# Two interleaved attention and gated-linear layers on one core: joint key/query weight loads, GpSimd alone for the key scaling, another engine order at the two layer changes

## The chip, the core and the metric

The kernel runs on 1 core of a Trainium2 chip. The metric is device microseconds of one execution. Five engines run their own instruction streams and meet at semaphores: TensorE (PE, with its weight loads shown as PEld), VectorE (DVE), ScalarE (ACT), GpSimd (POOL) and SyncE (SP), which issues the DMAs.

## What is computed

x is 2048 tokens by 576 features, in bf16. Two layers follow each other, with shared weights. Each is an attention half and a gated half, each behind a layer norm and with a residual:

```
qkv = ln(x) @ wqkv                       # 32 heads of 18
pq, pk = q @ w_phi, k @ w_phi            # per head
phi(p) = [softmax(p), softmax(-p)]       # 36 features per head
kv = sum over all tokens of phi_k * v ;  z = sum of phi_k
o  = (phi_q @ kv) / (phi_q @ z + 1e-6)
x  = x + o @ wo
x  = x + ((ln(x) @ w_gate) * (ln(x) @ w_up)) @ w_down      # 576 -> 4608 -> 576
```

The sum over all tokens makes a barrier in each layer: no token can get its attention output before the last token's key features are in.

## The kernel before

The tokens are 16 tiles of 128, in 8 blocks of 2. The program is recorded by a list scheduler written in Python (`Tracker`, `Sched`, lines 19 to 520): generators such as `t_ln` or `t_ain` yield groups of instructions, and the scheduler takes at each step the group with the smallest key, which is its estimated start less some constants (`bias`, `age`, `boost`). The engines then run exactly this order. Where a group may run on several engines (a request of the kind "alt"), the scheduler picks the engine that it believes will be done first.

The steps are these.

- **Head.** `t_load` loads the first tokens, `w_phi` and the raw key and query weights (`Wrawk`, `Wrawq`, five row blocks of 640 columns each). `t_fuse` transposes each row block (L954), copies it out (L957, tile `WTq`) and multiplies it by a block-diagonal of `w_phi` (L967), so that `Wk` and `Wq` give pk and pq at once. `t_flag` bounds the exponents from the Gram diagonals of the raw weights (L846, L849, L857, L863 to L866); every engine reads the flag and takes one of two programs (L231). These inputs take the fast program, which does not subtract a maximum ahead of exp.
- **Attention of layer 1.** For each tile: layer norm (`t_ln`: statistics L1007 and L1015 on DVE, the negated mean L1021, ln and exp on ACT L1023 and L1025, scaling L1036 on POOL or DVE, or L1032 on ACT), a transpose into `xT` (through PE at L1044 for the first block, through a DMA for the others), the projections to k and v (L1077), exp of p and of -p on ACT (L1198), the 64 sums on DVE (L1264), their reciprocals (two activations L1271, or L1267 on DVE), the scaling of the 1152 features by them in two halves (L1279, on POOL or on DVE), and the product with v (L1318) into two PSUM banks. `t_barrier` masks the result into `BD` (L1403).
- **Between barrier and gated half.** Tiles 0 and 1 go through the attention output (L1430 or L1439, L1460, L1468 to L1482, L1494, L1065), the layer norm and the transpose. The PE fills with query projections (`t_qproj`) of tiles 2 to 15, whose results lie in `xT` until their turn.
- **Gated half.** For each block 648 matmuls of 64 rows (L1599) and then 144 of the down projection (L1673, L1675); beside them lie the attention outputs of later blocks, and in layer 1 the keys of layer 2 for the blocks that are done (`t_ain(2, ..)`). Then the same barrier stands once more ahead of layer 2.

`proj` has two ways for a product with 576 weight rows: ten matmuls of 128 rows (L1065), or 18 of 64 rows (L1077), which go in pairs to the two halves of the array. Layer 1 takes the second way. In the second barrier the scheduler's own choice (a request "pe2") took the first.

`lend` lends feature tiles the memory of the down-projection buffers and of `hT`; so one tile carries several names (`dd`, `dd_h1g`, `dd_w3f`). The raw weights lie in memory that the gate and up weights take later (`over`), so the later loads wait for the fusing.

Of the kernel before, what the change touches and what calls it, by code (L numbers as in the profile page):

```python
# [6 lines left out]
BF16 = mybir.dt.bfloat16  # L7
# [10 lines left out]

class Tracker:
    def __init__(self):  # L20
        self.ops = {e: [] for e in ENGINES}
        self.count = {e: 0 for e in ENGINES}
        self.know = {e: {} for e in ENGINES}
        self.snap = {}
        self.fin = {}
        self.lastw = {}
        self.readers = {}
        self.lastacc = {}
        self.dma_groups = []
        self.pend_w = {}  # L30
        self.pend_r = {}
        self.stats = {"ops": 0, "waits": 0, "multiwait": 0, "pe_multiwait": 0}
# [66 lines left out]
    def _commit(self, me, eng, reads, writes, excl):  # L99
        for r in reads:  # L100
            d = self.readers.setdefault(r, {})
            if d.get(me[0], 0) < me[1]:
                d[me[0]] = me[1]
        for w in writes:
            self.lastw[w] = me
            self.readers[w] = {}
        for x in excl:
            self.lastacc.setdefault(x, {})[eng] = me[1]
# [135 lines left out]
class Op:  # L244
    __slots__ = ("dur", "emit", "reads", "writes", "excl", "mode", "order")

    def __init__(self, dur, emit, reads=(), writes=(), excl=(), mode=0, order=()):
# [9 lines left out]
class _Thread:  # L257
    __slots__ = ("gen", "prio", "req", "name", "deps_cache", "est", "t_ready", "seq", "alt", "boost", "age")
    _n = 0

    def __init__(self, gen, prio, name):
# [10 lines left out]
        self.age = 0.0  # L272


class Sched:

    def __init__(self, tracker):
        self.tr = tracker
        self.free_at = {e: 0.0 for e in ENGINES}
# [14 lines left out]
        self.hold = -1500.0  # L294
        self.alt_cost = {"dve": 1.0, "pool": 1.0, "act": 1.0}
# [17 lines left out]
    def _try_acquire(self, th):  # L313
# [4 lines left out]
        for i, t in self.pools["pb"]["rel_time"].items():  # L318
            self.pools["pb"]["rel_time"][i] = self.bank_time(i)
# [29 lines left out]
    def bank_time(self, bank):  # L349
        la = self.tr.lastacc.get(("pb", bank), {})  # L350
        return max([self.tr.fin.get(k, 0.0) for k in la.items()] + [0.0])

    def run(self):
        tr = self.tr
        while True:
# [83 lines left out]
            for th in self.threads:  # L439
                r = th.req  # L440
                if r[0] == "alt":
                    pick = None
                    for eng, ops in r[1]:
                        deps = []
                        for o in ops:
                            deps.extend(tr.deps_for(eng, o.reads, o.writes, o.excl, True, o.order))
                        e_ = max(self.free_at[eng], tr.ready_time(deps), th.t_ready)
# [5 lines left out]
                elif r[0] == "pe2":  # L453
                    ops = r[1 + self.pe_mode]
                    deps = []
                    for o in ops:
                        deps.extend(tr.deps_for("pe", o.reads, o.writes, o.excl, True, o.order))
                    est = max(self.free_at["pe"], tr.ready_time(deps, "pe"), th.t_ready)
                    th.alt = ("ops", "pe", ops, self.pe_mode)
                elif r[0] == "ops":  # L460
                    eng = r[1]
                    deps = []
                    for o in r[2]:
                        deps.extend(tr.deps_for(eng, o.reads, o.writes, o.excl, True, o.order))
                    est = max(self.free_at[eng], tr.ready_time(deps, eng), th.t_ready)
                    if eng == "pe" and r[2][0].mode != self.pe_mode:
                        est += self.pe_switch
                elif r[0] == "dma":
                    deps = tr.deps_for("sp", r[3], r[4], (), False)
                    est = max(self.free_at[r[9] if len(r) > 9 else "sp"], tr.ready_time(deps), th.t_ready)  # L470
# [3 lines left out]
                key = (est - self.bias.get(int(th.prio), 0.0) - th.age - (self.hold if late else th.boost), -th.prio)  # L474
# [8 lines left out]
            if r[0] == "ops":  # L483
# [4 lines left out]
                for o in r[2]:  # L488
# [11 lines left out]
                    t = fin  # L500
                if self.log is not None:
                    self.log.append((th.name, eng, t_beg, t, len(r[2]), self.free_at[eng]))
                self.free_at[eng] = t
            else:
# [4 lines left out]
                start = max(issue, self.dma_free[queue])  # L509
                xfer = nbytes / self.dma_bw  # L510
                self.dma_free[queue] = start + xfer
# [68 lines left out]
class K:  # L580
    def __init__(self, nc, A_x, A_wqkv, A_w_phi, A_wo, B_w_gate, B_w_up, B_w_down, out, fast, base=None):
# [10 lines left out]
        self.vlead = 9  # L592
        self.fage = 500.0
        self.fageq = 0.0
        self.fage2 = 300.0
        self.lnb = 2
        self.pes = (0, 1, 2, 3, 4, 5, 6, 7, 8, 9, 10, 11, 12, 13)
        self.early = (2, 2)
        self.pex = 1
        self.qlead = 12 if fast else 8  # L600
# [3 lines left out]
        self.lnlead = 7  # L604
# [4 lines left out]
        self.pqg = 6 if fast else 10  # L609
# [7 lines left out]
        self.fqp = 6.5  # L617
# [13 lines left out]
    def alloc(self):  # L631
# [25 lines left out]
        self.Wraw = {"k": AT("Wrawk", [128, 5, 640], BF16, wg0 + 6 * FF), "q": AT("Wrawq", [128, 5, 640], BF16, wu0 + 6 * FF)}  # L657
        self.WTq = AT("WTq", [128, 5, 5, 128], BF16, wu0 + 4 * FF)
# [29 lines left out]
        self.over = {("g", 3): [("Wraw", "k", kt) for kt in range(5)], ("u", 3): [("Wraw", "q", kt) for kt in range(5)], ("u", 2): [("WTq", i) for i in range(6)]}  # L688

    def lend(self):  # L690
# [63 lines left out]
        self.g_ot = [g("ot%d" % i) for i in range(self.NOT)]  # L754

# [78 lines left out]
    def t_flag(self):  # L834
# [5 lines left out]
        for i, which in enumerate("kq"):  # L840
            W = s.Wraw[which]
            gots = yield ("acqn", ["pb"], 2)
            banks = [g_[1] for g_ in gots]
            for kt in range(5):
                yield ("wait", ("ld", "raw", which, kt))
                yield ("ops", "pe", [Op(60, (lambda e, m=m, kt=kt, W=W, bank=banks[m // 3], c=128 * (m % 3), st=(kt == 0 and m in (0, 3)): e.matmul(  # L846
                    s.ps[:, bank, c:c + 128], W[:, kt, 128 * m:128 * m + 128], W[:, kt, 128 * m:128 * m + 128], start=st, stop=(kt == 4), skip_group_check=True)),
                    reads=[("Wraw", which, kt)], writes=[("pbd", banks[m // 3])], excl=[("pb", banks[m // 3])]) for m in range(5)])
            yield ("ops", "dve", [Op(d_dve(n), (lambda e, c=c, bank=bank, n=n: e.tensor_reduce(s.cst[:, c:c + 1], s.ps[:, bank, 0:n], AX.X, ALU.max)),  # L849
                                     reads=[("pbd", bank)], writes=[("cst", c)], excl=[("pb", bank)]) for c, bank, n in ((1, banks[0], 384), (2, banks[1], 256))]  # L850
                   + [Op(70, (lambda e: e.tensor_tensor(s.cst[:, 1:2], s.cst[:, 1:2], s.cst[:, 2:3], ALU.max)), reads=[("cst", 1), ("cst", 2)], writes=[("cst", 1)]),
                      Op(70, (lambda e, c=i: (e.tensor_copy(s.cst[:, 3:4], s.cst[:, 1:2]) if c == 0 else e.tensor_tensor(s.cst[:, 1:2], s.cst[:, 1:2], s.cst[:, 3:4], ALU.max))),
                         reads=[("cst", 1), ("cst", 3)], writes=[("cst", 3 if i == 0 else 1)])])
            for bank in banks:
                yield ("rel", "pb", bank)
        (_, bank), = yield ("acqn", ["pb"], 1)
        yield ("ops", "pe", [Op(250, (lambda e, c=c: e.matmul(s.ps[0:1, bank, 128 * c:128 * c + 128], s.cst[:, c:c + 1], s.identf[:], start=(c == 0), stop=(c == 1), skip_group_check=True)),  # L857
                                reads=[("cst", c), ("identf",)], writes=[("pbd", bank)], excl=[("pb", bank)]) for c in range(2)])
# [4 lines left out]
            Op(330, (lambda e: e.tensor_reduce(s.flg[0:1, 0:2], s.ps[0:1, bank, 0:256].rearrange("p (c n) -> p c n", c=2), AX.X, ALU.max)), reads=[("pbd", bank)], writes=[("flg", 0)], excl=[("pb", bank)]),  # L863
            Op(70, (lambda e: e.tensor_tensor(s.flg[0:1, 2:3], s.flg[0:1, 0:1], s.flg[0:1, 0:1], ALU.mult)), reads=[("flg", 0)], writes=[("flg", 1)]),
            Op(70, (lambda e: e.tensor_tensor(s.flg[0:1, 3:4], s.flg[0:1, 2:3], s.flg[0:1, 1:2], ALU.mult)), reads=[("flg", 0), ("flg", 1)], writes=[("flg", 2)]),
            Op(70, (lambda e: e.tensor_scalar(s.flag[0:1, 0:1], s.flg[0:1, 3:4], lim, None, ALU.is_lt)), reads=[("flg", 2)], writes=[("flag",)])])  # L866
# [4 lines left out]
    def t_load(self):  # L871
# [15 lines left out]
        def rawload(kt, queue="sp", which="k"):  # L887
            n = 128 if kt < 4 else 64
            c0 = D if which == "k" else 0
            return grp("raw%s%d" % (which, kt), [((lambda e, p=p: e.dma_start(s.Wraw[which][p:p + n, kt, :], wqkv[128 * kt:128 * kt + n, c0:c0 + 640])),  # L890
                                       [("Wraw", which, kt)], n * 640 * 2) for p in range(0, 128, n)], ("ld", "raw", which, kt), queue)

        yield from xload(0)
# [10 lines left out]
        def side():  # L904
            yield from grp("wphi5", items, ("ld", "wphi5"), "act")
            yield from rawload(1, "act")
            yield from rawload(3, "act")

        yield ("go", side(), 9, "side")
        yield from rawload(0)  # L910
        yield from rawload(2)
        yield from rawload(4)
        for kt in range(5):
            yield from rawload(kt, "sp", "q")
# [25 lines left out]
    def t_fuse(self, which):  # L940
        s = self
        Wm, km = (s.Wq, "Wq") if which == "q" else (s.Wk, "Wk")
        yield ("wait", "bdphi")
        yield ("age", s.fage if which == "k" else s.fageq)
        for kt in range(5):
            yield ("wait", ("ld", "raw", which, kt))
            if which == "q":
                yield ("wait", "branch")
                if not s.fast:
                    yield ("wait", ("ain", 1, s.fq + s.fqs * kt))  # L950
            if True:
# [998 lines left out]
```

## Time and profile before

| what | value |
|---|---|
| runs shown, median (lowest to highest of 3) | 1084.21 us (1083.66 to 1086.02) |
| the profiled execution's own time | 1083.22 us |
| its span, first to last instruction | 1081.5 us |
| PE busy | 1055.8 us, 98% |
| DVE, ACT, POOL busy | 487.3, 353.6, 198.6 us |
| first matmul of the gated half, layer 1 | at 104.56 us |
| last down projection of layer 1, first gated matmul of layer 2 | about 594.8 us, 625.74 us |
| granted TensorE clock, mean | 0.997 |

A window's row gives start and end, its length, then for PE, PEld, DVE, ACT and POOL the busy microseconds with the number of instructions in brackets, then the granted clock, the share of the DMA engines and GB/s. A row of the timeline gives start, duration, engine, line, operation, what is written from what, and the engine's idle time before it with what ended it. A row of the groups gives the count, the busy time with the mean duration in ns, and the idle time before.

### The profile page before, as it was taken

The page shows a single profiled execution, that of the slowest core. Times are in us where ns is not written, and L with a number is a line of the kernel's source. Part 1 is how long each engine was busy: PE and PEld are TensorE (multiplying, and loading weights), DVE is VectorE, ACT ScalarE, POOL GpSimd, SP SyncE. Part 2 cuts the span into 40 slices and gives each one's busy share as a digit, 9 for nine tenths or more (in the row PEclk, how much of TensorE's full clock was granted, in tenths as well). Part 3 has the DMA queues.
Part 4 walks back from the last instruction along what each step waited for, and adds up shares of the span by engine and source line. Part 5 has one row for each costly group of instructions (what it writes and reads, how often), then busy time and mean ns, then how long its engine had stood idle before and what let it go on. Part 6 is the DMA issues. An engine that isn't in the chain of part 4 may idle for free.

```text
span 1081.5 us, 34135 instructions
## 1 busy us (share of the span) xinstructions
PE 1055.8 (98%) x15678; PEld 807.8 (75%) x15678; DVE 487.3 (45%) x978; ACT 353.6 (33%) x846; POOL 198.6 (18%) x226
## 2 busy tenths in 40 slices
PE   6998999999999999999999999999999999999997
PEld 4666868879686877868686787777868686868684
DVE  5995626444453635425232644443424343424131
ACT  5786323314241432315141743131313131203030
POOL 3453003122130403103020220101010101000000
PEclk9999999999999999999999999999999999999999
DMA  5689155180835436183605133627190808180604
GB/s 141 120 220 289 37 144 127 54 192 15 219 40 176 83 100 149 33 200 37 199 14 165 45 47 83 175 61 196 37 220 21 237 15 232 25 221 15 209 2 146
DMA packets 179705, 128.18 MB, mean 119 GB/s; under 512 B 98016, under 2 KB 178400, under 8 KB 178400
## 3 DMA queue, kind: packets, MB, share of 16 engines
q1 hardware_dynamic: 178656, 125.55, 46.0%
q8 instruction: 125, 2.05, 0.8%
q10 hardware_dynamic: 896, 0.35, 0.1%
q14 instruction: 28, 0.23, 0.1%
HBM read 100.90 MB, written 2.36 MB: 95 GB/s over the span
## 4 chain that ended last, share of the span: by engine, by line
PE 90%; DVE 6%; DMA 2%; ACT 1%; issue 0%; POOL 0%; ACTq 0%
PE ps L1599 52%; PE ps L1673 22%; PE ps L1077 8%; PE ps L1675 3%; PE ps L1065 2%; DVE ss_w4f L1264 1%; DMA wdx<-in_B_w_down_dram 1%; PE ps L1460 1%; DVE dd_h1g L1279 1%; DVE st L1007 1%; PE ps L1318 1%; DMA wdr<-in_B_w_down_dram 0%; DMA Wrawk<-in_A_wqkv_dram 0%; DVE dd_w3f L1279 0%; DVE xln L1036 0%
## 5 line engine op out<-in xcount | busy, mean ns | idle before, releaser
L1599 PE MATMUL ps<-xT,Wg 64*128 64x256 bf16 x4608 | 582.9, 269 | 0.0
L1599 PE MATMUL ps<-xT,Wu 64*128 64x256 bf16 x4608 | 581.3, 269 | 0.2 <-DVE dd L1482 0.2
L1599 PEld LDWEIGHTS ps<-xT,Wu 64*128 64x128 bf16 x4608 | 431.7, 94 | 28.0 <-DVE dd L1482 0.4
L1599 PEld LDWEIGHTS ps<-xT,Wg 64*128 64x128 bf16 x4608 | 430.4, 94 | 28.7 <-issue 3.3
L1648 DVE TENSOR_TENSOR hT<-ps,hT 128x512 bf16<-128x512 f32 x288 | 199.2, 692 | 309.4 <-ACT hT L1646 309.4
L1646 ACT CAST hT<-ps 128x512 bf16<-128x512 f32 x288 | 168.6, 586 | 407.2 <-PE ps L1599 396.3
L1673 PE MATMUL ps<-wdr,hT 128*128 128x512 bf16 x960 | 244.5, 380 | 0.8 <-DMA wdr<-in_B_w_down_dram 0.5
L1279 POOL TENSOR_TENSOR dd<-dd,ss 128x576 bf16<-128x576 bf16 x94 | 111.2, 1210 | 456.6 <-ACT ss L1275 447.9
L1675 PE MATMUL ps<-wdr,hT 128*128 128x64 bf16 x960 | 184.9, 193 | 0.0
L1673 PEld LDWEIGHTS ps<-wdr,hT 128*128 128x128 bf16 x960 | 93.8, 98 | 112.0 <-DMA wdr<-in_B_w_down_dram 2.1
L1599 PE MATMUL ps<-xT,Wr 64*128 64x256 bf16 x1152 | 170.6, 269 | 0.0
L1036 POOL TENSOR_SCALAR xln<-x_sb,nmean,rstd 128x64 bf16<-128x64 bf16 (+1 forms) x98 | 60.1, 618 | 301.1 <-DVE nmean L1021 182.6
L1716 DVE TENSOR_TENSOR x_sb<-ps,x_sb 128x64 bf16<-128x64 f32 x32 | 7.0, 218 | 227.4 <-PE ps L1675 227.4
L1675 PEld LDWEIGHTS ps<-wdr,hT 128*128 128x128 bf16 x960 | 94.1, 98 | 0.2
L1275 ACT ACTIVATE ss<-ss 128x64 f32<-128x64 f32 x92 | 23.8, 259 | 193.1 <-DVE ss L1264 192.2
L1264 DVE TENSOR_REDUCE ss<-dd 128x64 f32<-128x1152 bf16 x48 | 63.6, 1346 | 23.7 <-ACT dd L1198 22.1
L1599 PEld LDWEIGHTS ps<-xT,Wr 64*128 64x128 bf16 x1152 | 66.9, 94 | 6.2
L1673 PE MATMUL ps<-wdx,hT 128*128 128x512 bf16 x192 | 54.4, 380 | 0.7 <-DMA wdx<-in_B_w_down_dram 0.5
L1077 PE MATMUL ps<-Wv,xT 64*128 64x288 bf16 x540 | 47.8, 287 | 3.2 <-DVE flag L866 1.3
L1077 PE MATMUL ps<-Wk,xT 64*128 64x288 bf16 x540 | 47.6, 287 | 1.2 <-ACT dd_w3f L1198 0.8
L1007 DVE BATCH_NORM_STATS2 st<-x_sb 128x6 f32<-128x288 bf16 x120 | 46.3, 444 | 0.7 <-DVE flag L866 0.7
L1077 PE MATMUL ps<-Wo,oT 64*128 64x288 bf16 x504 | 40.2, 283 | 0.0
(129 smaller groups left out, 752.1 us busy)
## 6 DMA issues: line engine op xcount, KB each, us to landing
wdr<-in_B_w_down_dram SPq DMA_DIRECT2D x240, 288.0 KB, 3.7
wdx<-in_B_w_down_dram SPq DMA_DIRECT2D x48, 288.0 KB, 3.8
Wg<-in_B_w_gate_dram SPq DMA_DIRECT2D x4, 1152.0 KB, 13.6
Wu<-in_B_w_up_dram SPq DMA_DIRECT2D x4, 1152.0 KB, 15.9
x_sb<-in_A_x_dram SPq DMA_DIRECT2D x8, 288.0 KB, 4.4
out_dram<-x_sb SPq DMA_DIRECT2D x16, 144.0 KB, 2.4
xT<-xln SPq DMA_TRANSPOSE x56, 2.7
Wrawq<-in_A_wqkv_dram SPq DMA_DIRECT2D x4, 160.0 KB, 4.8
```

Of the source, the lines that this page charges most:

```text
L1007: ops.append(Op(d_dve(288), (lambda e, j=j, h=h, src=src: e.bn_stats(st[:, sl[j], 6 * h:6 * h + 6], src)), reads=rd, writes=[("st", sl[j], ...
L1036: em = [(lambda e, j=j, a=a, b=b, c=c: e.tensor_scalar(xln[:, sl[j], a:b], x_sb[:, ss[j], c:c + b - a], s.nmean[:, sl[j]:sl[j] + 1], rstd[ ...
L1065: full = [Op(d_pe(N), (lambda e, k=k, h=h: e.matmul(s.ps[:, banks[h], 0:N], L[:, k, :], Wm[:, k, N * h:N * h + N], start=(k == 0 and fresh ...
L1077: out.append(Op(61, (lambda e, h=h, k=k, st=(i == 0 and k == 0), sp=(i == 1 and k == 3): e.matmul(s.ps[:, banks[h], 0:N], L[r, k, :], Wm[r ...
L1264: Op(1265, (lambda e: e.tensor_reduce(ss[:, sm, :], e4, AX.X, ALU.add)), reads=s.ddk(sm, 0) + s.ddk(sm, 1), writes=[("ss", sm)]),
L1275: yield ("ops", "act", [Op(200, (lambda e, kw=kw: e.activation(ss[:, sm, :], ss[:, sm, :], **kw)), reads=[("ss", sm)], writes=[("ss", sm)])])
L1279: yield ("alt", [(eng, [Op(dur, (lambda e, ev=ev, rb=rb: e.tensor_tensor(ev, ev, rb, ALU.mult)), reads=s.ddk(sm, br) + [("ss", sm)], write ...
L1599: out.append(Op(54.3, (lambda e, bank=bank, cs=cs, lhsT=lhsT, rhs=rhs, st=st, sp=sp: e.matmul(ps[:, bank, cs].rearrange("p (a n) -> p a n" ...
L1646: yield ("ops", "act", [Op(480, (lambda e, gb=gb, p=p: e.copy(hT[:, p, :], ps[:, gb, :])), reads=[("gu", gb)], writes=[("hT", p)] + (s.raw ...
L1648: yield ("ops", "dve", [Op(600, (lambda e, ub=ub, p=p: e.tensor_tensor(hT[:, p, :], ps[:, ub, :], hT[:, p, :], ALU.mult)), reads=[("gu", u ...
L1673: ops = [Op(d_pe(512), (lambda e: e.matmul(s.ps[:, bank, 0:512], lhsT, s.wslot(slot)[:, fi, 0:512], start=(f == 0), stop=(f == NF - 1))), ...
L1675: Op(d_pe(64) + 3, (lambda e: e.matmul(s.ps[:, z, 64 * sl:64 * sl + 64], lhsT, s.wslot(slot)[:, fi, 512:576], start=(f == 0 and (sl == 0 o ...
```

## The change

- The raw key and query weights become one tile `Wraw` of 1216 columns, loaded by row block with one DMA instead of two (block 4 in two halves); `x` of tiles 0 and 1 is loaded tile by tile, tile 1 behind two weight blocks. The keys' and the queries' transposed copies get separate buffers (`WT`), and the five key blocks are fused as five parallel threads (`t_fuse1`). The Gram products of both go into the same pair of banks; the flag takes one reduction less.
- Tiles 0 and 1 are normed one by one; block 1 too is transposed through PE (`pex` 2), and block 2 may be normed ahead of the flag (`lnb` 3). In layer 1 the negated mean is made on ACT from block 1 on, and the scaling of the norm no longer has ACT as a choice.
- In `softmax_tail` of the fast program, tiles 0 to 13 have their key features scaled on POOL alone, and the last two on DVE alone (`crit` 2).
- Around the second barrier, `rowfirst` gives the projections the 64-row way until block 0 of layer 2 is ready.
- The scheduler gets a model of a lock between DVE and POOL (`port`), start times, one common DMA clock, changed constants, and a table `AGES` with a constant for each of 62 threads.

```diff
+AGES = {
+    "ain1_10": -143, "ain1_12": -228, "ain1_13": 255, "ain1_14": 386, ...
+}
...
-        self.free_at = {e: 0.0 for e in ENGINES}
+        self.free_at = {e: 800.0 for e in ENGINES}
+        self.port = {"dve": 0.0, "pool": 0.0}
...
+    def port_time(self, eng, op, t):
+        if eng == "pool":
+            return max(t, self.port["dve"])
+        if op.port:
+            return max(t, self.port["pool"])
+        return t
...
-                key = (est - self.bias.get(int(th.prio), 0.0) - th.age - (self.hold if late else th.boost), -th.prio)
+                key = (est - self.bias.get(int(th.prio), 0.0) - th.age - th.age0 - (self.hold if late else th.boost), -th.prio)
...
-        self.vlead = 9
-        self.fage = 500.0
+        self.vlead = 5
+        self.row2 = True
+        self.fage = 300.0
-        self.lnb = 2
+        self.lnb = 3
-        self.pex = 1
-        self.qlead = 12 if fast else 8
+        self.pex = 2
+        self.qlead = 8 if fast else 8
-        self.lnlead = 7
+        self.lnlead = 8
-        self.pqg = 6 if fast else 10
+        self.pqg = 8 if fast else 10
...
-        self.Wraw = {"k": AT("Wrawk", [128, 5, 640], BF16, wg0 + 6 * FF), "q": AT("Wrawq", [128, 5, 640], BF16, wu0 + 6 * FF)}
-        self.WTq = AT("WTq", [128, 5, 5, 128], BF16, wu0 + 4 * FF)
+        self.Wraw = AT("Wraw", [128, 5, 2 * D + 64], BF16, wg0 + 4 * FF)
+        self.WT = {w: AT("WT" + w, [128, 5, 5, 128], BF16, wu0 + 4 * FF + 6400 * i) for i, w in enumerate("kq")}
...
+    def rowfirst(self, L):
+        return L == 1 or (self.fast and self.row2 and ("xTB", 2, 0) not in self.sc.events)
...
-        yield from xload(0)
+        yield from x0load(0)
+        yield from rawload(0, ["sp"])
+        yield from rawload(2, ["sp"])
+        yield from x0load(1)
+        yield from rawload(4, ["sp", "sp"])
-        yield from rawload(0)
-        yield from rawload(2)
-        yield from rawload(4)
-        for kt in range(5):
-            yield from rawload(kt, "sp", "q")
...
+        if boot:
+            yield ("ops", "act", [Op(150, (lambda e: e.activation(s.nmean[:, s0:s1], mean2, ACTF.Copy, scale=-1.0)), reads=key("mv"), writes=key("nmean"))])
+        else:
+            yield ("ops", "dve", [neg])
...
-                           for eng, dur in (("pool", (800, 200)[:2 - fast]), ("dve", (400,) if fast else (400, 200)))[:1 + (fast or boot)]] + ([("act", act)] if boot else []))
+                           for eng, dur in (("pool", (620, 200)[:2 - fast]), ("dve", (400,) if fast else (400, 200)))[:1 + (fast or boot)]])
...
-        yield from s.proj(st_, Wm, km, banks, rowmode=crit > 0 and ev[1] == 1)
+        yield from s.proj(st_, Wm, km, banks, rowmode=crit > 0 and s.rowfirst(ev[1]))
...
-        yield from s.proj(st_, s.Wq, "Wq", banks, rowmode=L == 1)
+        yield from s.proj(st_, s.Wq, "Wq", banks, rowmode=s.rowfirst(L))
...
-                           for eng, dur in (("pool", 1150), ("dve", 675))[:1 + (crit > 1 or crit and s.fast)]])
+                           for eng, dur in ((("pool", 1150), ("dve", 675))[crit > 1:1 + (crit > 1)] if s.fast else (("pool", 1150), ("dve", 675))[:1 + (crit > 1)])])
...
-            yield from s.proj(st_, s.Wv, "Wv", banks, rowmode=L == 1)
+            yield from s.proj(st_, s.Wv, "Wv", banks, rowmode=s.rowfirst(L) and (L == 1 or st_ >= NS - 2))
```

## The prediction, made before the changed kernel was run

> **What bounds the kernel now.** I read first the busy times by stage, then in the long stage the groups by engine, then the timeline of the scaling and of the flag.
>
> ```profile
> core 0: us, PE busy (x) PEld busy (x) DVE busy (x) ACT busy (x) POOL busy (x), PEclk, DMA share, GB/s
> 0.00:17.60 17.60, 10.08 (x115) 8.19 (x116) 8.12 (x31) 7.61 (x15) 5.39 (x17) 1.00 0.73 200
> 17.60:86.10 68.50, 60.50 (x878) 41.95 (x879) 64.65 (x107) 55.08 (x176) 36.09 (x35) 0.98 0.65 170
> 86.10:104.56 18.46, 17.69 (x230) 11.54 (x228) 11.43 (x25) 13.04 (x37) 6.37 (x6) 1.00 1.07 305
> 104.56:594.84 490.28, 489.38 (x7452) 381.11 (x7447) 211.77 (x427) 148.17 (x350) 97.05 (x111) 1.00 0.45 109
> 594.84:625.74 30.90, 29.46 (x279) 22.53 (x278) 20.11 (x47) 22.24 (x60) 9.09 (x7) 1.00 0.15 39
> 625.74:1081.50 455.76, 448.67 (x6737) 342.44 (x6736) 171.20 (x345) 107.44 (x213) 44.60 (x52) 1.00 0.45 115
> ```
>
> Rows 4 and 6 are the gated halves, 946 us of 1081.5, with PE busy without a gap; nothing in the change shortens their matmuls. All there is to win lies in rows 1 to 3 (104.56 us) and in row 5 (30.9 us). "Busy" overstates PE where matmuls wait inside their pipeline, so I price PE by distances of starts in the trace: a 64-row matmul of 288 columns every 61.4 ns (36 in 2.21 us in a dense stretch), a 128-row one every 122.6 ns, 56 ns for a transpose, and 97 ns more whenever a 64-row matmul follows a 128-row one or the reverse (215 ns in place of about 120, 152 in place of 56). By these prices PE has 55.0 us of work in row 2 (38 of these switches included), 15.4 in row 3, 487.8 in row 4, 27.6 in row 5. So PE has 13 us to spare in row 2, and DVE, busy for 64.65 of 68.5 us, sets its length.
>
> ```profile
> L1264 DVE TENSOR_REDUCE ss_w4f<-dd_h1g 128x64 f32<-128x1152 bf16 x12 | 16.0, 1340 | 0.0
> L1279 DVE TENSOR_TENSOR dd_h1g<-dd_h1g,ss_w4f 128x576 bf16<-128x576 bf16 x13 | 15.5, 1200 | 0.3 <-ACT ss_w4f L1271 0.2
> L1279 DVE TENSOR_TENSOR dd_w3f<-dd_w3f,ss_w4f 128x576 bf16<-128x576 bf16 x4 | 5.0, 1240 | 0.0
> L1036 DVE TENSOR_SCALAR xln<-x_sb,nmean,rstd 128x576 bf16<-128x576 bf16 x6 | 4.0, 673 | 0.1
> L1036 DVE TENSOR_SCALAR xln<-x_sb,nmean,rstd 128x64 bf16<-128x64 bf16 x6 | 2.1, 349 | 0.2
> ...
> L1279 POOL TENSOR_TENSOR dd_h1g<-dd_h1g,ss_w4f 128x576 bf16<-128x576 bf16 x11 | 16.7, 1525 | 13.9 <-ACT ss_w4f L1271 12.5 <-DVE ss_w4f L1267 1.3
> ```
>
> Of DVE's 64.65 us, 20.5 are the 17 key scalings that fell to it, and they are dear because POOL does the other half at the same time:
>
> ```profile
> 34.21 1.19 POOL L1279 TENSOR_TENSOR dd_h1g<-dd_h1g,ss_w4f 128x576 bf16<-128x576 bf16 x1
> ...
> 53.76 0.76 DVE L1279 TENSOR_TENSOR dd_h1g<-dd_h1g,ss_w4f 128x576 bf16<-128x576 bf16 x1 [0.22 <-ACT ss_w4f L1271]
> 53.80 1.76 POOL L1279 TENSOR_TENSOR dd_h1g<-dd_h1g,ss_w4f 128x576 bf16<-128x576 bf16 x1 [3.25 <-ACT ss_w4f L1271]
> ```
>
> Alone, POOL needs 1.19 us and DVE 0.76; together the second waits for the first, so the pair takes 1.8 us. At 34.21 POOL's instruction ran beside DVE statistics and lost nothing. So the split saves little (1.8 against 2.4 us) and costs the bound engine 1.2 us each time.
>
> ```profile
> 16.72 0.14 DVE L866 TENSOR_SCALAR flag<-flg 1x1 int32<-1x1 f32 x1
> 17.60 0.67 PE L1077 MATMUL ps<-Wv,xT 64*128 64x288 bf16 x8 [1.30 <-DVE flag L866]
> ...
> 85.71 0.69 PE L1318 MATMUL ps<-vx_h2g,dd_h1g 128*128 128x76 bf16 x13 [2.12 <-POOL dd_h1g L1279]
> ```
>
> Every engine stops at the flag until 17.6; the last key product before the barrier waited 2.12 us for the scaling.
>
> **The change part by part.** Instruction counts of the changed program are by its order on each engine.
>
> *Loads and flag.* The twelve weight loads that the trace shows landing from 4.62 to 10.77 us become six; SP issues the last at about 4.0 instead of 6.1 us (0.5 us each). Bytes are nearly the same (1216 columns for 1280) and the last 0.83 MB came at 286 GB/s, so I let the last land at about 9.5 us. Behind it stand ten Gram matmuls (0.56), the two reductions (0.89 by L849), three fp32 products, one reduction of 384 (0.41 measured for 256, about 0.5) and three small ones (0.15 each): flag at about 13.3, branch at 14.1. That is 3.5 us earlier than 17.6. Four of five key blocks are fused ahead of it, three before; the first value projections move behind it (0.6 us of PE, which has room). Bounds: 1.5 us, if landing is limited by the bytes and DVE's copies stand in front of the reductions; 4.5 if the longer rows load faster.
>
> *Scaling on POOL alone.* DVE, row 2: minus 17 scalings (-20.5), plus 4 for the last two tiles (4 x 0.76 = +3.0), six negated means to ACT (6 x 0.16 = -1.0), two more statistics (+0.8), four more xln of 576 and three of 64 columns (4 x 0.673 + 3 x 0.349 = +3.7), a copy, a cast and a reciprocal more (+0.45, +0.45, +0.55). 64.65 becomes 52.1. POOL: 19 scalings (27.6) become 32 (28 key, 4 query) at 1.187 = 38.0, and two xln of 576 and three of 64 fewer (-3.0): 36.1 becomes 43.5. ACT: six means at 0.295 (the nearest row, L1030), two xln groups less (-2.8), some copies less (-1.5): 55.1 becomes 52.6. PE: 53.9 with 44 switches. Four engines between 43 and 54 us: the new bound is all of them.
>
> What the DVE sum leaves out is the lock: each of its 19 xln instructions may find POOL inside a scaling. POOL will be busy some 0.7 of the time, and the mean wait inside is 0.6 us, so 0.42 each; the trace's own means (673 where 424 is the median) hold half of that. I add 4 us: 56. Divided by the fill that DVE had as the bound (64.65 / 68.5 = 0.944) this is 59.4; with four engines nearly level, each waiting for the others in a fixed order, I take 62, 6.5 us less than 68.5. Bounds: 55.2 (52.1 / 0.944) and 67. Block 1's transpose through PE helps at the start of this: its keys' projection waited until 27.12 for a DMA issued at 23.81.
>
> [...] The rows give 1.187 to 0.758, 1.57 times. POOL's first scaling comes some 9 us after the branch (8 statistics, 4 aggregates, the norms, the first sum: 6.7 + 1.34 + 0.55 on DVE and ACT), at 23. [...]
>
> *First barrier to gated half.* PE's work is 16.0 us for 15.4. The second tile's transposes now stand ahead of the barrier, where its product at 92.54 had waited for them, and more queries fill the end. 18.46 becomes 17.2, -1.2 (bounds 0 and -2.4). The scaling of the last tiles is 1.5 us on DVE for 1.8 split; that is inside the 62.
>
> *Weights of the gated half.* The last of them landed at 95.99, 26.4 us after the first was issued, 3 us behind the last norm of block 7. In the new order eight sums still stand behind that norm; it should lie near 58, the weights be there near 88, and the half starts at 76.1 + 17.2 = 93.3. They are hidden, with 5 us to spare. This is what comes next if the stage shrinks further.
>
> *64-row products in the second barrier.* 15 projections change from ten at 122.6 to 18 at 61.4: 1.226 to 1.105, -1.8 us. But row 5 had no switch inside and now has 15 (15 x 0.097 = +1.5). [...] The 3.3 us of waiting shrink by the shorter scaling (-0.3) and by 4.5 us of queries in front of the key product that waited 0.77: I take 2.5. 30.9 becomes 29.1, -1.8 (bounds 0 and -3).
>
> *Gated halves.* One switch and 26 matmuls more: 488.3 for 487.8 and 447.6 for 447.2, +0.9. The tail is the same, instruction for instruction.
>
> Sum: -3.5 - 6.5 - 1.2 - 1.8 + 0.9 = -12.1, made against the profiled execution's own 1083.22 us: 1071.1. The median of the runs shown is 1 us above that execution, so I say 1071.
>
> **The rivals.**
>
> - *The engines overlap as well as DVE did alone* (stretch 56, flag 4 earlier, the barriers -2 and -2.5): -12.5 - 4 - 4.5 + 0.9 = -20, 1063. For it: each engine's sum is below 54. Against it: four level engines seldom fill each other's gaps.
> - *The lock gives the gain back*: DVE's norms queue behind POOL and the sums behind them, stretch 67, so -1.5 - 3.5 - 3 + 0.9 = -7, 1076. For it: xln of up to 1.29 us and POOL scalings of up to 1.78 stand in the trace. Against it: sums and statistics, two thirds of DVE's new work, showed no such stretching.
> [...]
> - *No change*: the order model hides one wait and opens another of the same size.
>
> **How the numbers follow.** Forecast 0.52 (1067 to 1075), the full overlap 0.15, the lock 0.20, slower 0.09, no change 0.04. A measurement of this kernel can tell about 0.2%, 2 us, from nothing. Faster is 0.52 + 0.15 + 0.20 = 0.87. The range takes in the overlap case and the lock case with a few us for their own bounds, 1061 to 1081, and leaves out most of the slower case.
>
> **What would show it right or wrong.** Right: the flag near 13 us, DVE without a key scaling until the last two tiles, POOL's scalings at 1.2 to 1.3 us in the mean, `BD` written at 72 to 79, the gated half starting at 90 to 97, 30.9 us between the layers down to 28 to 30, gated halves the same within 1 us. Wrong: POOL's scalings above 1.5 in the mean, or PE's start of the gated half waiting for `Wg` or `Wu`; a second barrier longer than 31 us would say that the switches cost more than 97 ns.

## The result and the profile after

The changed kernel takes 1075.6 us (median of 4 runs, 1072.6 to 1077.14) where the kernel before takes 1083.93 us beside it: a ratio of 0.9917, with a 95% interval of 0.989 to 0.9944. The profiled execution took 1074.8 us with a span of 1073.0 us, against 1083.22 and 1081.5 before. The forecast was 1071.0, with a range of 1061 to 1081.

The same six stages as before, in the profile of the changed kernel (columns as before: start and end, length, busy time of PE, PEld, DVE, ACT and POOL, granted clock, DMA share, GB/s):

```profile
0.00:17.60 17.60, 10.10 (x117) 8.58 (x117) 8.85 (x27) 7.04 (x17) 3.94 (x16) 1.00 0.68 195
17.60:81.05 63.45, 59.33 (x855) 41.43 (x856) 56.15 (x99) 48.43 (x164) 42.93 (x43) 0.97 0.65 184
81.05:98.72 17.67, 16.97 (x239) 12.16 (x237) 12.15 (x26) 14.30 (x37) 3.75 (x4) 1.00 0.79 282
98.72:589.48 490.76, 489.85 (x7462) 381.26 (x7458) 211.68 (x428) 148.27 (x354) 100.87 (x114) 1.00 0.45 110
589.48:617.31 27.83, 27.79 (x404) 19.78 (x405) 20.64 (x46) 19.33 (x55) 0.82 (x1) 1.00 0.11 34
617.31:1073.05 455.74, 448.08 (x6746) 342.70 (x6746) 174.01 (x350) 108.69 (x215) 49.20 (x56) 1.00 0.45 116
```

Set against the six rows of before, the lengths change by 0.0, -5.05, -0.79, +0.48, -3.07 and -0.02 us, together -8.45, which is the difference of the two spans to 0.05 us. (The border between rows 4 and 5 stands 0.16 us earlier in the row of before; drawn at the end of the last down projection in both, these two rows change by +0.32 and -2.91.) The gain lies in the long stretch and in the second barrier, with 0.8 us in the first barrier; the head gave nothing.

Of the groups of the long stretch, by engine, the key scaling (L1342) and the work that meets it (count, busy time, mean ns of one, idle before and what ended it):

```profile
L1342 POOL TENSOR_TENSOR dd_h1g<-dd_h1g,ss_w4f 128x576 bf16<-128x576 bf16 x20 | 23.3, 1192 | 8.8 <-ACT ss_w4f L1334 8.8
L1327 DVE TENSOR_REDUCE ss_w4f<-dd_h1g 128x64 f32<-128x1152 bf16 x10 | 13.4, 1336 | 1.9 <-ACT dd_h1g L1261 1.8
L1099 DVE TENSOR_SCALAR xln<-x_sb,nmean,rstd 128x576 bf16<-128x576 bf16 x10 | 6.6, 656 | 1.5 <-ACT rstd L1089 1.5
L1342 POOL TENSOR_TENSOR dd<-dd,ss 128x576 bf16<-128x576 bf16 x4 | 5.6, 1416 | 3.9 <-ACT ss L1338 3.9
L1099 DVE TENSOR_SCALAR xln<-x_sb,nmean,rstd 128x64 bf16<-128x64 bf16 x9 | 4.9, 549 | 0.3
L1342 DVE TENSOR_TENSOR dd_w3f<-dd_w3f,ss_w4f 128x576 bf16<-128x576 bf16 x4 | 3.8, 1002 | 0.1
```

POOL's key scalings fell from 1525 to 1192 ns in the mean, DVE kept the four of the last two tiles, and POOL now idles for ACT's reciprocals: it isn't the bound. DVE, which before had no idle time in front of its sums, now waits there for the exponentials of ACT. In the head, the steps that lead to the flag:

```profile
7.53 0.71 PE L1012 MATMUL ps<-ident,Wraw 128*128 128x128 bf16 x5 [1.49 <-DMA Wraw<-in_A_wqkv_dram]
...
10.20 1.10 PE L893 MATMUL ps<-Wraw 128*128 128x128 bf16 x10
11.14 0.46 PE L1025 MATMUL ps<-BDphi,WTk 128*128 128x144 bf16 x6
11.43 0.44 PE L1012 MATMUL ps<-ident,Wraw 128*128 128x128 bf16 x5
11.95 0.32 PE L1025 MATMUL ps<-BDphi,WTk 128*128 128x108 bf16 x3
12.11 0.72 PE L893 MATMUL ps<-Wraw 128*128 128x128 bf16 x10
12.66 0.44 PE L1012 MATMUL ps<-ident,Wraw 128*128 128x128 bf16 x5
12.98 0.32 PE L1025 MATMUL ps<-BDphi,WTk 128*128 128x144 bf16 x3
13.14 0.72 PE L893 MATMUL ps<-Wraw 128*128 128x128 bf16 x10
...
13.79 0.89 DVE L896 TENSOR_REDUCE cst<-ps 128x1 f32<-128x384 f32 x2
...
16.77 0.14 DVE L910 TENSOR_SCALAR flag<-flg 1x1 int32<-1x1 f32 x1
...
17.64 0.31 PE L1025 MATMUL ps<-BDphi,WTk 128*128 128x144 bf16 x3 [1.72 <-DVE flag L910]
```

The last row block was issued 2.8 us earlier than before (at 3.26 for 6.08 us) but landed only 0.34 us earlier (at 10.43 for 10.77): between the first and the last landing of these weights the DMA engines were busy throughout in both programs (a share of 1.01 and 297 GB/s now, 1.06 and 286 before). Its ten Gram products (L893) ran only at 13.14. PE hardly waited in between: it was busy for 2.63 of these 2.71 us, with work of other row blocks that stands in front. The flag was written at 16.91 us where it was written at 16.86 before.

### The profile page after: what moved, and what is told of

It is laid out like the page before. It is cut to its first block, busy times and chain, and to the rows that moved or that the text cites. A ratio compares the mean times of both kernels' runs of the same rounds, so it can differ in the third digit from the quotient of the medians.

```text
span 1073.0 us, 34366 instructions
## 1 busy us (share of the span) xinstructions
PE 1052.1 (98%) x15812; PEld 805.9 (75%) x15812; DVE 483.5 (45%) x974; ACT 346.1 (32%) x838; POOL 201.5 (19%) x232
## 3 DMA queue, kind: packets, MB, share of 16 engines
q8 instruction: 126, 2.06, 0.8%
## 4 chain that ended last, share of the span: by engine, by line
PE 93%; POOL 2%; DVE 2%; DMA 1%; ACT 1%; issue 0%; ACTq 0%
PE ps L1662 53%; PE ps L1736 23%; PE ps L1140 10%; PE ps L1738 3%; PE ps L1523 1%; POOL dd_w3f L1342 1%; DMA wdx<-in_B_w_down_dram 1%; PE ps L1381 1%; PE ps L1128 1%; DVE xln L1099 1%; POOL dd_h1g L1342 1%; DMA Wraw<-in_A_wqkv_dram 1%; DVE ss_w4f L1327 0%; PE ps L1107 0%; POOL dd L1342 0%; PE ps L893 0%
## 5 line engine op out<-in xcount | busy, mean ns | idle before, releaser
L1662 PEld LDWEIGHTS ps<-xT,Wu 64*128 64x128 bf16 x4608 | 432.1, 94 | 27.4 <-DVE x_sb L1777 0.3
L1342 POOL TENSOR_TENSOR dd<-dd,ss 128x576 bf16<-128x576 bf16 x92 | 107.5, 1194 | 414.9 <-ACT ss L1338 414.9
L1099 POOL TENSOR_SCALAR xln<-x_sb,nmean,rstd 128x64 bf16<-128x64 bf16 (+1 forms) x94 | 57.5, 617 | 340.7 <-DVE nmean L1080 157.9
```

The lines of the kernel that those rows point to most:

```text
L1099: em = [(lambda e, j=j, a=a, b=b, c=c: e.tensor_scalar(xln[:, sl[j], a:b], x_sb[:, ss[j], c:c + b - a], s.nmean[:, sl[j]:sl[j] + 1], rstd[ ...
L1342: yield ("alt", [(eng, [Op(dur, (lambda e, ev=ev, rb=rb: e.tensor_tensor(ev, ev, rb, ALU.mult)), reads=s.ddk(sm, br) + [("ss", sm)], write ...
L1662: out.append(Op(54.3, (lambda e, bank=bank, cs=cs, lhsT=lhsT, rhs=rhs, st=st, sp=sp: e.matmul(ps[:, bank, cs].rearrange("p (a n) -> p a n" ...
```

## The experiments

The theory: the stretch shrank because DVE lost 13 of its 17 scalings, and the flag stayed late because of its place in PE's order. The rivals: the new order made the gain and not the engine; the fusing of the key blocks, not the flag, decides when the keys' projection can begin. Every edit below is one line, but the list scheduler plans the rest of the program anew after it. So each run is read stage by stage. `BD` stands for the start of the first of its two writes; the second starts 0.5 us behind it, but 6.7 us behind it in a_flag800. Times of two events, lengths of three stages (the second barrier from the end of the last down projection to the first gated matmul) and the end of the span, in us:

| kernel | flag written | first key projection | branch to `BD` | `BD` to gated half | second barrier | end of span |
|---|---|---|---|---|---|---|
| before | 16.86 | 21.70 | 68.50 | 18.46 | 30.74 | 1081.5 |
| changed | 16.91 | 21.78 | 63.41 | 17.67 | 27.83 | 1073.0 |
| b_pool | 16.60 | 21.43 | 65.28 | 18.46 | 30.58 | 1076.9 |
| a_split | 18.97 | 22.31 | 64.44 | 32.95 | 28.17 | 1088.0 |
| a_flag800 | 17.09 | 23.55 | 68.46 | 27.73 | 28.05 | 1088.0 |
| a_flag1500 | 14.11 | 21.90 | 72.09 | 18.42 | 28.05 | 1079.9 |

**b_pool: before, with the scaling on POOL alone.**

```diff
-  for eng, dur in (("pool", 1150), ("dve", 675))[:1 + (crit > 1 or crit and s.fast)]])
+  for eng, dur in ((("pool", 1150), ("dve", 675))[crit > 1:1 + (crit > 1)] if s.fast else ...)])
```

> The kernel before with one line of the change: in layer 1 the key scalings of tiles 0 to 13 go to POOL alone, those of tiles 14 and 15 to DVE alone (DVE carries 4 key scalings ahead of the first barrier where it carried 17). Loads, fuse threads, flag, norms, constants and the second barrier stay as before. Theory A (freeing DVE of the scaling is what shortened the long stretch): from the branch to the last write of BD 63 to 65 us where before had 68.5, POOL's scalings 1.2 us in the mean, the second barrier still 30.5 to 31, in all 1078 to 1080.5. Rival B (the gain came from the new order of fuse, norms and projections, and the scheduler of before, which knows nothing of the lock, cannot use it): stretch 67 to 69, 1083 to 1085. Rival C (POOL becomes the bound, or DVE's norms queue behind it): stretch above 70, 1086 or more.

Measured: 1079.0 us, ratio to before 0.9962 (0.9949 to 0.9975). The rows of its stretch, first barrier and second barrier, and two of the groups in the stretch:

```profile
17.33:82.61 65.28, 60.22 (x888) 42.58 (x889) 54.89 (x95) 53.11 (x174) 46.96 (x48) 0.97 0.71 179
82.61:101.07 18.46, 17.11 (x220) 11.13 (x217) 11.43 (x25) 13.23 (x37) 6.36 (x6) 1.00 0.94 301
...
590.81:621.39 30.58, 29.46 (x280) 22.52 (x278) 21.51 (x49) 22.24 (x60) 5.58 (x5) 1.00 0.15 40
```

```profile
L1279 POOL TENSOR_TENSOR dd_h1g<-dd_h1g,ss_w4f 128x576 bf16<-128x576 bf16 x20 | 23.3, 1188 | 10.0 <-ACT ss_w4f L1271 10.0
...
L1036 DVE TENSOR_SCALAR xln<-x_sb,nmean,rstd 128x576 bf16<-128x576 bf16 x8 | 6.0, 746 | 0.3 <-ACT rstd L1025 0.2
```

Theory A holds: one line takes DVE in the stretch from 64.65 to 54.89 us busy and the stretch from 68.50 to 65.28, with the old loads, fuse threads and constants. The stretch is 0.3 us above what A gave and 1.7 below what B gave; the total lies inside A's range. That is 3.2 of the 5.1 us that the whole change gained there. (The planner moved other work too after this edit, two more of the long norm scalings to DVE for example, so the 3.2 us are those of the line with its replanning.) The barriers stay within 0.2 us of before, so their gains (0.8 and 2.9) come from other parts. POOL's mean is 1188 ns, it was busy for 46.96 of the 65.28 us, and the stretch is below the 70 of rival C. The lock may be seen where the norms are: xln of 576 columns rose from 673 to 746 ns in the mean on DVE, 0.6 us over eight of them.

**a_split: the changed kernel, with the scaling on either engine again.** The edit is the same line the other way round.

> The changed kernel with that one line put back: the key scalings of layer 1 may go to POOL or DVE as the scheduler sees it (its lock model stays), 15 of 32 fall to DVE. Theory A: the stretch from branch to BD grows from 63.4 to 66.5 to 68.5, DVE busy in it back above 62 us, 1078.5 to 1081 against 1075.6 for the changed kernel. Rival B: stretch within 1 us of 63.4, 1075 to 1077. Flag (16.9) and second barrier (27.8) unchanged by both.

Measured: 1088.54 us, ratio to before 1.0042 (1.0028 to 1.0056), 13 us above the changed kernel and outside what either theory said. The stretch and the first barrier, and PE's rows in the barrier:

```profile
19.70:84.14 64.44, 59.49 (x855) 41.14 (x856) 61.49 (x101) 49.62 (x166) 37.71 (x37) 1.00 0.66 179
84.14:117.09 32.95, 26.34 (x331) 18.20 (x328) 17.04 (x37) 20.47 (x57) 10.99 (x10) 0.90 0.62 180
```

```profile
94.48 4.73 PE L1140 MATMUL ps<-Wq,xT 64*128 64x288 bf16 x72
99.14 0.57 PE L1107 MATMUL ps<-ident,xln 128*128 128x128 bf16 x6
99.65 4.24 PE L1140 MATMUL ps<-Wq,xT 64*128 64x288 bf16 x62
103.82 0.90 PE L1523 MATMUL ps<-BD,eT 128*128 128x76 bf16 x20
107.71 0.86 PE L1557 MATMUL ps<-ident,dd 128*128 128x128 bf16 x6 [3.00 <-DVE dd L1545]
```

DVE's load in the stretch came back nearly as foreseen (61.49 us for 56.15; above 62 was expected), yet the stretch grew by 1.0 us only, which is rival B's number. But the changed kernel lost 1.5 us to a low clock at the start of its stretch, as the last section shows, and this run didn't; counted from the first key projection, the stretch is 61.8 us against 59.3, +2.6. What cost 15 us is the first barrier. The attention product of the second tile (L1523) stands in PE's order behind 134 query matmuls; after it PE waits 3.00 us for DVE, a spell at half clock begins (from 106.94 to 113.77 us), and all that follows is late. The gated half then took 486.8 us instead of 490.8, with some 140 matmuls fewer in it, so 4 us came back. This run doesn't decide between A and B for the stretch. It shows that the undone line and the order can't be pulled apart when the planner orders everything anew: here the new order around the barrier cost more than the edit.

**a_flag800 and a_flag1500: the changed kernel, with the flag's groups preferred.**

```diff
-        self.fage2 = 300.0
+        self.fage2 = 800.0      # a_flag1500: 1500.0
```

> The changed kernel with the flag thread's constant 800 in place of 300, which moves its Gram products ahead: the last ten stand before all but one of the key products of the fusing, where they stood behind seven groups that wait for ACT's and DVE's copies. Theory A (the flag was late because of its place in PE's order, not of the loads): flag written at 14 to 15.5 us in place of 16.9. If the start of the program is bound by the flag, BD and all behind it move by the same 1.5 to 3 us, 1072.5 to 1074.5. Rival B (the head is bound by the fusing of the five key blocks, the flag only stands beside it): flag earlier by as much, but the first projection of keys stays at 21.5 to 22.5 us, BD within 1 us of 81, 1075 to 1077. Rival C (the loads limit the flag): flag at 16.5 or later.

Measured: 1089.54 us, ratio to before 1.0052 (1.0039 to 1.0066), slower than either total that was given. The flag wasn't earlier (17.09), which is rival C's number, although its last Gram products stood before all but one key product: the loads landed up to 1.1 us later than in the changed kernel's execution (the last at 11.21), and PE ran at about half its later pace until about 12.8 us, ten Gram products taking 1.07 us instead of 0.56, so that the last ten started at 13.77. This execution can't tell the two apart. Of the 15 us between the two spans, 10 lie behind the first write of `BD` and 5 in the stretch. PE's order there, and what DVE waited for:

```profile
86.18 6.32 PE L1140 MATMUL ps<-Wq,xT 64*128 64x288 bf16 x98
92.43 0.52 PE L1381 MATMUL ps<-vx_h2g,dd_h1g 128*128 128x95 bf16 x8
...
92.98 0.55 DVE L1466 TENSOR_TENSOR BD<-ps,maskf 128x380 bf16<-128x380 f32 x1 [6.15 <-PE ps L1381]
```

Eight key products, half a microsecond of work, stand behind 98 query matmuls, and the second half of `BD` waits 6.15 us for them. Later in this barrier PE waits 2.56 and 4.73 us for the norms of the two tiles, and a spell of 10.24 us at half clock begins at 108.38.

> As the run before with the constant at 1500: the last Gram products stand behind the Gram products of the other blocks and one group of five transposes only, and all key products of the fusing behind the branch. Theory A: flag at 13.2 to 14.2 us (last block landed at 10.4, Gram 0.7, reductions 0.9, three products 0.8, small ones 1.1); if the flag binds, BD 2.5 to 3.5 us earlier than 81, 1072 to 1074. Rival B (fusing binds): flag just as early, but with all key products behind the branch the first projection of keys comes at 22 to 24, BD at 81 to 83, 1075.5 to 1078.

Measured: 1082.86 us, ratio 0.9992 (0.9977 to 1.0008): no gain over before is left. Its head and its stretch, and two waits of PE in the stretch:

```profile
0.00:14.84 14.84, 6.68 (x67) 5.85 (x67) 5.94 (x21) 4.05 (x8) 4.19 (x16) 1.00 0.74 211
14.84:86.93 72.09, 63.15 (x906) 44.78 (x907) 53.17 (x99) 53.92 (x174) 46.34 (x49) 0.95 0.61 172
```

```profile
70.31 0.79 PE L1140 MATMUL ps<-Wk,xT 64*128 64x288 bf16 x10 [1.57 <-DMA xT<-xln]
72.41 3.27 PE L1140 MATMUL ps<-Wk,xT 64*128 64x288 bf16 x26 [1.31 <-DMA xT<-xln]
```

The flag came at 14.11, inside the 13.2 to 14.2 expected: with its Gram products in front it needs 4.1 us from the last landing (10.05), where the changed kernel needed 6.5. So the flag was late by its place in the order. But the first key projection stands at 21.90 where it stood at 21.78: the key products of the fusing, now behind the branch, take up the time won. They do so although PE kept its full clock from the branch up to there (1.00 in the column), while the changed kernel lost 1.5 us to half clock. An earlier flag alone was worth nothing to the keys. That is theory B, up to this point. The 65.0 us from there to `BD` (59.3 in the changed kernel) neither theory had: PE waits for transposes of the normed tiles that land late (1.57 and 1.31 us above), and spends two spells of 3.41 us at half clock, from 27.74 and from 72.11.

No run here holds the whole order fixed and changes the engine, the row mode or the flag alone. Such a run would separate the remaining 1.9 us of the stretch, and the mode from the order in the second barrier; it was not tried. Each program has one profile, too, so that what varies from execution to execution is seen only across programs.

## Why the prediction was right, and where it was not

The measured 1075.6 us lies inside the range, 4.6 us above the forecast. By the profiles the change gained 8.45 us where the sum had 12.1. Of the 3.65 us that are missing, 3.5 are the flag's. The misses of the other terms (+1.45 in the stretch, +0.41 in the first barrier, -1.11 in the second, -0.60 in the gated halves) nearly cancel, and that they do is luck.

- **What bounds the kernel**: right. Rows 4 and 6 moved by 0.3 to 0.5 and by 0.02 us; all the gain is in the stages named.
- **Loads and flag, -3.5: this step failed; it measured 0.0.** The flag was put at 13.3 us and written at 16.91, 3.6 later. 0.9 of that is the landing, guessed at 9.5 us and measured at 10.43: the earlier issue did little with the DMA engines full already, a case that the step had only in its lower bound. The other 2.7 us are what the step left out, the order of PE: it let the ten Gram products start at the landing, but a Gram group, transposes and key products of other blocks stood before them until 13.14, and until 11.03 a Gram product started every 107 ns where the sum had 56. From the Gram products to the flag it was right, 3.77 us for 3.8. a_flag1500 shows that the flag can stand at 14.1 when they are in front. It also points to the second fault of the step: it took the flag for the start of the keys' work, where the fusing has to be done as well.
- **Stretch, -6.5: the mechanism right, measured -5.05.** DVE was put at 56 us busy and was 56.15, POOL at 43.5 and was 42.93, ACT at 52.6 and was 48.43. The term that was mis-sized is the fill: DVE filled 0.885 of the stretch (56.15 / 63.45), where 0.903 (56 of 62) had been allowed. A spell at half clock behind the branch, told below, cost 1.5 us up to the first key projection, the size of the miss; but the stretch of before has a spell of the same length (from 27.4 us), so what the spells are worth in the difference stays open. The lock's 4 us were too many: 19 xln took 11.5 us where the old means give 9.9, and the four DVE scalings took 1.0 more than the 3.0 of the sum, 2.6 together. So DVE's total came out right by 1.4 us that the sum had nowhere, which is luck.
- **The price of a scaling on POOL, 1.187 us by the rows**: right. A key scaling cost 1.19 us on POOL, 1.57 times DVE's 0.76 alone, and POOL had 20 us to spare in the stretch (busy for 42.93 of 63.45).
- **First barrier, -1.2: measured -0.79.** b_pool, which has the other parts of the program as before, has the old 18.46.
- **Weights of the gated half, hidden**: right. They landed at 89.94 us, 8.8 us before the half started. (The 76.1 of the prediction is the branch at 14.1 and the stretch of 62.)
- **Second barrier, -1.8: measured -2.9, by the term that was mis-sized, the waiting.** The 29.1 us were 26.6 of PE's work and 2.5 of waiting. No run shows the 26.6 by itself: it is an estimate, the instructions of the changed kernel's stage at the trace's distances of starts (61.4, 122.6 and 56 ns, about 40 for the attention products, 97 a switch), which give 27.6 for before; the whole stage was measured at 27.83. By this estimate the time above PE's work was 3.1 to 3.3 and is 1.2 (27.83 - 26.6): PE's rows of before show waits of 0.77, 0.26 and 0.41 us for the scaling, for `BD` and for the first quotient, and those of after show none. More queries stand in front of each. Before, then after:

```profile
609.21 0.69 PE L1318 MATMUL ps<-vx,dd 128*128 128x76 bf16 x13 [0.77 <-POOL dd L1279]
...
611.59 0.50 PE L1460 MATMUL ps<-BD,eT 128*128 128x95 bf16 x9 [0.26 <-DVE BD L1403]
...
613.73 0.57 PE L1494 MATMUL ps<-ident,dd 128*128 128x128 bf16 x6 [0.41 <-DVE dd L1482]
```

```profile
598.56 4.70 PE L1140 MATMUL ps<-Wq,xT 64*128 64x288 bf16 x74
603.19 0.86 PE L1381 MATMUL ps<-vx,dd 128*128 128x76 bf16 x18
603.98 2.38 PE L1140 MATMUL ps<-Wq,xT 64*128 64x288 bf16 x36
606.29 0.54 PE L1523 MATMUL ps<-BD,eT 128*128 128x76 bf16 x10
```

  The price of a mode change held: 36 matmuls of 64 rows take 2.31 us from their start to the next, 0.10 more than at 61.4 ns each. The whole stage is 27.8 to 28.2 us in all four programs with the changed kernel's mode and order there, and 30.58 in b_pool with neither. That the order did most and the mode little is read from the trace and its prices, not shown by a run.
- **Gated halves, +0.9: measured +0.3 to +0.5**, by the border that is taken.
- **The rivals.** Full overlap (1063) needed the flag 4 us earlier and didn't come. The lock's rival gave 1076, close to the median, but by a stretch of 67 us; the stretch was 63.4. POOL as the bound is out: its scalings stand at 1.19 us, and it idles for 20 us of the stretch. So the total lies between the forecast and that rival for a reason that neither gave, the flag.

## What to carry to other kernels

When an engine bounds a stage, giving a whole class of its work to a slower idle engine can pay even at 1.57 times the price per instruction (in b_pool the stretch went from 68.50 to 65.28 us); check the slower engine's start, count and mean against the stage's end. A load that is issued earlier need not land earlier (here 2.8 us at the issue became 0.34 at the landing, with the DMA engines full, a share of 1.01), and an early landing helps only if its consumers stand early in their engines' orders (here the last block landed at 10.43 us and its Gram products ran at 13.14): walk each queue from the landing to the last consumer and count what stands between. And where a planner rewrites the order, one line or one constant can cost 10 to 15 us at the next barrier (a_split, a_flag800), so read such an experiment by stage and not only by its total.

## What the runs showed of the hardware that was not expected

PE's clock. In the first microseconds of the changed kernel's profile, matmuls of 128 columns start every 107 ns, and from about 11.1 us on every 56 ns, while the profile's clock column says 1.00 for both. Later falls do show in the column. These are windows from the wait for the flag on, of the changed kernel and then of a_split, which has the same PE instructions in the same order up to the first key projection:

```profile
16.00:18.00 2.00, 0.36 (x5) 0.29 (x7) 1.19 (x6) 0.40 (x1) 0.33 (x2) 0.96 0.00 0
18.00:20.00 2.00, 2.00 (x18) 1.18 (x16) 2.00 (x7) 0.70 (x2) 0.55 (x3) 0.50 0.00 0
20.00:22.00 2.00, 2.00 (x24) 1.32 (x24) 1.09 (x7) 1.45 (x5) 0.00 (x0) 0.68 0.00 0
```

```profile
18.00:20.00 2.00, 0.29 (x5) 0.23 (x7) 1.19 (x5) 0.34 (x1) 0.27 (x2) 1.00 0.00 0
20.00:22.00 2.00, 2.00 (x33) 1.43 (x34) 2.00 (x7) 1.40 (x4) 0.61 (x3) 1.00 0.00 0
```

Both had waited 1.72 us for the flag. The changed kernel then ran at half clock from 17.86 to 21.27 us and needed 4.14 us from the branch to the first key projection; a_split kept its clock and needed 2.61. So the spell cost 1.5 us. In the head it was the other way round: a_split stayed at 107 ns until about 14.8 us, and its flag, in an identical order, came 2.06 us later. Of this, 1.1 us are there already at the second Gram group (9.14 for 8.04 us), by a weight block that landed 1.1 us later; the other 0.95 us arise up to the last Gram group (15.20 for 13.14), mostly while a_split is still at 107 ns and the changed kernel at 56.

Besides the one at the program's end, the six profiles have nine spells at half clock: seven are 3.41 us long and the others 6.83 (a_split) and 10.24 (a_flag800), once, twice and three times the same length. In the changed kernel and in before the spell starts 6.83 and 17.07 us behind the moment at which the head's distances fall from 107 to 56 ns (11.03 and 10.34 us), two and five times 3.41. In the 3.41 us ahead of its spell PE was busy for 1.69 us in the changed kernel and for 1.52 in before; a stretch of this length in before with 1.59 us (from 82.0) had no spell behind it. What brings a spell on isn't shown by these runs.

So the same PE instructions differed by about 1 us in the head and by 1.5 us behind the branch from one execution to another, beside what the loads did. Such differences may also be why the times of one kernel spread over 4 us and more (1072.6 to 1077.14 for the changed one); no run shows it. Before and b_pool had their spell at 27 us, behind a wait of PE of 1.9 us for ACT; in the changed kernel that wait is gone, and the spell fell behind the branch instead.
